# Attention scores as two float16 products over 128 rows instead of one float32 product over 64 rows, from the fourth chunk on

## The chip, the cores and the metric

The kernel runs on one core of a Trainium2 chip. Its metric is the device time in microseconds (us) of one execution; less is better. Before the change three runs gave 695.9, 698.4 and 699.2 us, with a median of 698.4 us. The five engines that matter are TensorE (PE, with its weight loads listed apart as PEld), VectorE (DVE), ScalarE (ACT), GpSimd (POOL) and SyncE (SP), which here only issues DMAs.

## The reference

Attention with a local window and a few global keys, and then a feed-forward layer with a gate:

```python
scores = scale * np.matmul(q, k.transpose(0, 1, 3, 2))      # q, k, v: 4 x 8 x 768 x 64
scores = scores - slopes[:, None, None] * dist               # dist: distance to the key
scores = np.where(is_global | is_local, scores, -1e9)        # 8 global keys, 96 local ones
a = softmax(scores)
x = (a @ v), heads side by side                              # 3072 x 512
h = x @ w_in                                                 # 512 x 2048
out = (h * tanh(softplus(h))) @ w_out                        # 2048 x 512
```

## The kernel before, in words

The 3072 rows are cut into 12 chunks of 256 rows (3 to each of the 4 batches). A chunk's attention consists of 8 tasks t; one task is a pair of heads for one block of 128 rows. The 8 tasks of a chunk fall into two groups G of 4 tasks (4 heads each), and q and k are loaded group by group (`load_qk`). A task runs through these steps, with the lines of the profile:

- scores (`scores`, L340): PE multiplies q and k of the two heads. The heads lie on partitions 0 to 63 and 64 to 127, the operands are float32, and each head's result goes to its own PSUM tile (`sc0`, `sc1`), of which there is one each. A task sees 256 keys (own block, previous 96 keys, global keys); the first block of a batch sees 128.
- `largest` (L354, DVE): adds the mask `mb` or `mb0`, takes the row maximum and writes A. `exps` (L363, ACT): the exponential.
- `high_a` and `low_a` (L147 on DVE or L149 on ACT, and L153, mostly on POOL): A is split into a high and a low float16 part, `hl`, so that later products need only float16. `turn_a` (L383): a DMA on SP transposes `hl` into `AT`. There are three `hl` buffers, so an `hl` can be written only when the transpose of three tasks earlier has read its own.
- `weigh` (L399, PE): AT times v, two tasks later, into `pav` (in the third chunk into `po`).

When the 8 tasks of a chunk are done, `rows` (L410, DVE) divides by the sum, `high_x` and `low_x` (L421, DVE) split the result, and `turn_x` (L427, SP) transposes it into `xT`.

The feed-forward layer has 8 steps m for each chunk: 24 matmuls of 256 columns (`ph`, L444), a chain of ACT and DVE operations (L451, L455, L459, L463, L467, L471, L475), a split of the result into `gt` (L149, then L153 on POOL), and, two steps later, 12 matmuls of 512 columns (`po`, L493). All these operands are float16 in high and low parts, three products for one.

The order of the work is fixed in two ways. Up to step 23 or so a string, PROGRAM, lists every operation by a letter and a number; all engines, SP among them, take it in that order, and each engine works strictly in its own order. In it `q` is a load of q and k, `X` a transposing DMA of `hl`, `t` is `largest`, `g` is `high_a`, `Q` frees `po`, and `W` is `weigh`. Behind it a loop (`attend`) emits the rest in a simple order, and a scheduler places it on the engines.

Of the kernel before, what the change touches and what calls it, by code (L numbers as in the profile page):

```python
# [11 lines left out]
F16 = mybir.dt.float16  # L12
# [4 lines left out]
ALU = mybir.AluOpType  # L17
# [11 lines left out]

SV = 256.0  # L30
# [84 lines left out]
def windowed(st, tc, loc):  # L115
# [14 lines left out]

    cp = st.enter_context(tc.tile_pool(name="cp", bufs=1))
# [24 lines left out]
    raw = {}  # L156
    vraw = {}
# [3 lines left out]
    def load_qk(G):  # L161
        if G >= 2 * NC:
            return
        ci, g = divmod(G, 2)
        b, c = divmod(ci, NCHB)
        qr = raws.tile([P, GH // 2, CH], F32, name="qr", bufs=4)
        kr = raws.tile([P, GH // 2, KW], F32, name="kr", bufs=4)
        o = OWN if c == 0 else 0
        pairs = slice(g * GH // 2, (g + 1) * GH // 2)
        nc.sync.dma_start(qr, L.qT[b].rearrange("(a j) d s -> (j d) a s", j=2)[:, pairs, c * CH:(c + 1) * CH])  # L170
        for j in range(2):
            half = slice(j * D, (j + 1) * D)
            nc.sync.dma_start(kr[half, :, o:], L.kd[ci, half].rearrange("p (a j) w -> p a j w", j=2)[:, pairs, j, o:])
        raw[G] = (qr, kr)
# [68 lines left out]
    def mask_far(h, other=False):  # L243
        copy(mb[:, h, :], rel, -L.slopes[h] * UNIT, other)

# [86 lines left out]
    def scores(t):  # L332
        ci, g, blk, a2, first, nk = shape(t)
        qr, kr = raw[2 * ci + g]
# [3 lines left out]
        for j in range(2):  # L338
            half = slice(j * D, (j + 1) * D)
            nc.tensor.matmul(sc[j][:, 0:w], qr[half, a2, blk * P:(blk + 1) * P], kr[half, a2, col0:col0 + w], start=True, stop=True)  # L340
        pend[t] = sc

    def largest(t):
# [7 lines left out]
        for j in range(2):  # L351
            h = g * GH + 2 * a2 + j
            m = mb0[:, h, :] if first else mb[:, h, :]
            nc.vector.tensor_tensor_reduce(out=A[:, j, 0:w], in0=sc[j][:, 0:w], in1=m, scale=-1.0 / UNIT, scalar=3.0e38, op0=ALU.add, op1=ALU.min, accum_out=nm[:, h:h + 1])  # L354
# [159 lines left out]
    def flags():  # L514
# [12 lines left out]
        "h": high_v, "l": low_v, "x": window_v,  # L527
# [20 lines left out]
        s17 l3 t17 G12 g16' H12 p16' y17 E30 E31 Z6 i7 s18 o6 g17 t18 s19 j7 z12 m7 u7 y18 i13 g18 n7 r7 v4 x3 X16 p17 X17 q7 Z12 p18 X18 t19 s20  # L548
        y19 G7 H7 j13 z7 t20 Z7 m13 u13 g19 y20 p19' o12 s21 o7 i14 n13 g20 t21 s22 r13 y21 g21 X19 G13 p20' H13 t22 Q0 y22 p21 q8 z13' g22' p22'
# [243 lines left out]
```

## Time and profile before

| what | us |
|---|---|
| median of the three runs | 698.4 |
| the profiled execution | 697.84 |
| its span on the core | 695.7 |
| matmul busy (PE) | 630.9 |
| ACT busy | 472.6 |
| DVE busy | 449.2 |
| POOL busy | 266.3 |

The time of an execution is the span from the first to the last instruction and some 2 us around it. In the span matmuls overlap each other, so the mean of one matmul record is longer than the step from one to the next; where a length is needed, the starts of consecutive rows are taken. A row of the timeline gives the start, the length, the engine, the line, what is written from what is read, how many instructions were merged, and in brackets the idle time before it with what ended it. In the groups, "x" is a count, "|" stands ahead of busy us and the mean ns of one.

### The profile page before, as it was taken

To read this page: it belongs to the slowest core of one execution; us is meant where nothing else is said; L and a number is where in the kernel's file an instruction comes from. 1 tells how busy PE (TensorE), PEld (TensorE's weight loads), DVE (VectorE), ACT (ScalarE), POOL (GpSimd) and SP (SyncE) were. 2 spreads that over 40 slices of the span, in tenths; PEclk is the share of its full clock that TensorE was granted. 3 is DMA by queue.
4 is the path that set the end of the run, shared out by engine and by line. 5 is a ranking of instruction groups with operands and counts; after the bars stand their busy time and mean duration, and the time that the engine had idled before them with its cause. 6 is when DMAs were issued, how large, how long until landed. Compare 5 with 4: busy or idle time off the path is not lost.

```text
span 695.7 us, 13412 instructions
## 1 busy us (share of the span) xinstructions
PE 630.9 (91%) x4898; PEld 407.1 (59%) x4898; DVE 449.2 (65%) x1129; ACT 472.6 (68%) x1034; POOL 266.3 (38%) x222
## 2 busy tenths in 40 slices
PE   5556886799799999999999999999999999999993
PEld 3334554456377566666666666666666666666661
DVE  6699989976568647557556566566466565554441
ACT  6576686687577577776776776776776777765652
POOL 1456545642252244344334443443334433331120
PEclk9957899999899999999999999999999999999997
DMA  8999864456444437734435434554444324230000
GB/s 209 201 267 260 255 216 136 149 115 132 108 125 89 116 107 152 144 91 112 116 94 119 96 104 91 118 113 100 109 93 85 69 61 61 77 48 15 31 1 35
DMA packets 152681, 80.38 MB, mean 116 GB/s; under 512 B 121376, under 2 KB 141856, under 8 KB 152608
## 3 DMA queue, kind: packets, MB, share of 16 engines
q1 hardware_dynamic: 152608, 79.46, 48.5%
q8 instruction: 40, 0.66, 0.4%
q14 instruction: 33, 0.27, 0.1%
HBM read 38.54 MB, written 6.29 MB: 64 GB/s over the span
## 4 chain that ended last, share of the span: by engine, by line
ACT 32%; DVE 31%; PE 21%; issue 10%; DMA 4%; POOL 2%; SPq 1%; DVEq 0%; POOLq 0%; ACTq 0%
PE ph L444 9%; DVE e L455 8%; PE po L493 7%; ACT r L463 6%; DVE r L471 6%; ACT u L459 5%; ACT r L467 5%; ACT gt L149 5%; ACT e L451 4%; ACT A L363 3%; DVE gf L475 3%; DVE ws L295 3%; PE sc L340 2%; DVE ws L294 2%; PE pav L493 2%
## 5 line engine op out<-in xcount | busy, mean ns | idle before, releaser
L444 PE MATMUL ph<-xT,wts 128*128 128x256 f16 x2304 | 275.0, 277 | 18.2 <-DVE gmax L475 14.2
L444 PEld LDWEIGHTS <-wts 128*128 128x128 f16 x2304 | 223.9, 99 | 55.2 <-issue 18.5
L493 PE MATMUL po<-wts,gt 128*128 128x512 f16 x1056 | 244.7, 381 | 4.2 <-ACT gt L149 2.7
L153 POOL TENSOR_TENSOR hl<-A,hl 128x512 f16<-128x512 f32 (+1 forms) x90 | 106.6, 1185 | 268.9 <-issue 127.4
L493 PEld LDWEIGHTS <-gt 128*128 128x128 f16 x1152 | 112.3, 99 | 127.6 <-issue 6.4
L153 POOL TENSOR_TENSOR gt<-gf,gt 128x512 f16<-128x512 f32 x93 | 119.6, 1286 | 117.6 <-ACT gt L149 108.6
L471 DVE TENSOR_TENSOR r<-r,e 128x512 f32<-128x512 f32 x96 | 71.8, 748 | 113.3 <-ACT r L467 113.1
L459 ACT ACTIVATE u<-e 128x512 f32<-128x512 f32 x96 | 60.3, 628 | 97.6 <-DVE e L455 97.6
L363 ACT ACTIVATE A<-A,nm 128x256 f32<-128x256 f32 (+1 forms) x192 | 92.0, 480 | 31.2 <-DVE nm L354 30.9
L455 DVE TENSOR_SCALAR e<-e 128x512 f32<-128x512 f32 x96 | 75.7, 789 | 48.6 <-ACT e L451 48.0
L354 DVE CUSTOM_DVE_ANT_0 A<-sc,mb 128x256 f32<-128x256 f32 (+1 forms) x192 | 71.8, 395 | 50.7 <-PE sc L340 48.5
L340 PE MATMUL sc<-kr,qr 64*128 64x256 f32 (+1 forms) x384 | 77.6, 453 | 21.5 <-DVE nm L354 15.7
L149 ACT ACTIVATE gt<-gf 128x512 f16<-128x512 f32 x91 | 57.1, 627 | 40.4 <-DVE gmax L475 40.1
L340 PEld LDWEIGHTS sc<-kr,qr 64*128 64x128 f32 x384 | 37.7, 205 | 58.7 <-DVE nm L354 22.8
L463 ACT ACTIVATE r<-u,quarter 128x512 f32<-128x512 f32 x96 | 69.0, 719 | 2.4
L475 DVE CUSTOM_DVE_ANT_0 gf<-r,ph 128x512 f32<-128x512 f32 x96 | 65.5, 682 | 4.7 <-DVE r L471 2.1
L467 ACT ACTIVATE r<-r 128x512 f32<-128x512 f32 x96 | 60.3, 628 | 2.5
L451 ACT ACTIVATE e<-ph 128x512 f32<-128x512 f32 x96 | 55.8, 581 | 6.8 <-PE ph L444 6.6
L399 PEld LDWEIGHTS <-AT 128*128 128x128 f16 x1056 | 37.8, 100 | 38.2 <-issue 21.0
L153 POOL TENSOR_TENSOR wts<-ws,wts 128x512 f16<-128x512 f32 x32 | 42.0, 1322 | 30.7 <-ACT wts L149 27.1
L399 PE MATMUL pav<-vc,AT 128*128 128x64 f16 x432 | 32.0, 198 | 12.6 <-DMA AT<-hl 11.6
L147 DVE TENSOR_SCALAR hl<-A 128x512 f16<-128x512 f32 (+1 forms) x72 | 36.5, 507 | 4.4 <-ACT A L363 1.9
(82 smaller groups left out, 392.4 us busy)
## 6 DMA issues: line engine op xcount, KB each, us to landing
wts<-w_in SPq DMA_DIRECT2D x16, 512.0 KB, 5.2
wts<-w_out SPq DMA_DIRECT2D x15, 512.0 KB, 5.6
kr<-kd SPq DMA_DIRECT2D x32, 208.0 KB, 3.8
qr<-qT SPq DMA_DIRECT2D x24, 256.0 KB, 3.2
vr<-v SPq DMA_DIRECT2D x12, 512.0 KB, 4.8
out<-ob SPq DMA_DIRECT2D x11, 512.0 KB, 2.9
vc<-vo SPq DMA_DIRECT2D x20, 192.0 KB, 2.8
kr<-kd SPq DMA_DIRECT2D x16, 144.0 KB, 4.0
```

Of the source, the lines that this page charges most:

```text
L149: nc.scalar.activation(out, in_, AF.Copy, scale=scale)
L153: (nc.vector if other else nc.gpsimd).tensor_tensor(out, in_, high, op=ALU.subtract)
L340: nc.tensor.matmul(sc[j][:, 0:w], qr[half, a2, blk * P:(blk + 1) * P], kr[half, a2, col0:col0 + w], start=True, stop=True)
L363: nc.scalar.activation(A[:, j], A[:, j], AF.Exp, bias=nm[:, h:h + 1], scale=-1.0, accum_out=rs[:, h:h + 1])
L444: nc.tensor.matmul(ph[:, j, :].rearrange("p (b t) -> p b t", b=2), wv4[:, 2 * fb, x, c * P:(c + 1) * P], xT[:, :, y * NCC + c, :], start=( ...
L455: nc.vector.tensor_scalar(e, e, NTOP, 0.5, op0=ALU.min, op1=ALU.add)
L459: nc.scalar.activation(u, mish[m]["e"], AF.Square)
L463: nc.scalar.activation(mish[m]["r"], mish[m]["u"], AF.Ln, bias=quarter, scale=1.0 / RS)
L467: nc.scalar.activation(r, r, AF.Exp, scale=-1.0)
L471: nc.vector.tensor_tensor(r, r, mish[m]["e"], op=ALU.mult)
L475: nc.vector.tensor_tensor_reduce(out=gf, in0=mish[m]["r"], in1=mish[m]["h"], scale=SG / (SV * SW * RS), scalar=0.0, op0=ALU.mult, op1=ALU. ...
L493: nc.tensor.matmul(pos[ci][t], gt[:, x, j, t * P:(t + 1) * P], wv4[:, 2 * fb + 1, y, :], start=(fb == 0 and n == 0), stop=(fb == NFB - 1 a ...
```

## The change

From the fourth chunk on (`CF32 = 3`; tasks 24 to 95, groups 6 to 23) the scores are made of float16 products. q and k of a head are loaded twice, onto partitions 0 to 63 and 64 to 127 (`qd`, `kd`, which hold both copies in memory). q, times 256, is split so that the upper copy keeps the high float16 part and the lower copy the rest (`qs`); k is split into a high part `kh` and a rest `kl`, each on all 128 partitions. One matmul over 128 partitions with `kh` then gives (high + low of q) times high of k, and a second one with `kl` is added to it in PSUM. The masks are multiplied by 256 once (`units`, N in PROGRAM), since the scores are. The first three chunks keep the float32 form.

Each group so gets five operations more: `high_q` (a in PROGRAM), `low_q` (b, DVE), `high_k` (c), and `low_k` in two halves (d and e, 832 columns each). Behind PROGRAM `high_q` is on ACT, `high_k` on DVE, and `low_k` on POOL. The PSUM tiles change too: both heads' scores lie in one tile `sc`, and there are two such tiles in place of one pair. The float32 buffers `qr` and `kr` are now two of twice the size in place of four, and a group's load is one DMA for q and one for k, each with twice the bytes.

```diff
+    CF32 = 3
...
+        qr = raws.tile([P, GH, CH], F32, name="qr")
+        kr = raws.tile([P, GH, KW], F32, name="kr")
+        nc.sync.dma_start(qr, L.qd[ci, :, g * GH:(g + 1) * GH, :])
+        nc.sync.dma_start(kr[:, :, o:], L.kd[ci, :, g * GH:(g + 1) * GH, o:])
+        split[G] = (qr, kr) + tuple(stk.tile([P, GH, n], F16, name=m) for m, n in (("qs", CH), ("kh", KW), ("kl", KW)))
...
+    def low_q(G):
+        qr, qs = split[G][0], split[G][2]
+        nc.vector.scalar_tensor_tensor(qs[D:P], qr[D:P], SQ, qs[D:P], op0=ALU.mult, op1=ALU.subtract)
...
+    def split_qk(G):
+        if CF32 <= G // 2 < NC:
+            high_q(G)
+            high_k(G, True)
+            low_q(G)
+            low_k(G, 0, False)
+            low_k(G, 1, False)
...
+        for m in (mb0, mb):
+            nc.vector.tensor_scalar(m, m, SQ, None, op0=ALU.mult)
...
-        sc = [ps.tile([P, W], F32, name=f"sc{j}", bufs=1) for j in range(2)]
-        for j in range(2):
-            half = slice(j * D, (j + 1) * D)
-            nc.tensor.matmul(sc[j][:, 0:w], qr[half, a2, blk * P:(blk + 1) * P], kr[half, a2, col0:col0 + w], start=True, stop=True)
...
+            both = ps.tile([P, 2, W], F32, name="sc")
+            sc = [both[:, j] for j in range(2)]
+            for j in range(2):
+                hh = 2 * a2 + j
+                for n, kk in enumerate((kh, kl)):
+                    nc.tensor.matmul(sc[j][:, 0:w], qs[:, hh, blk * P:(blk + 1) * P], kk[:, hh, col0:col0 + w], start=(n == 0), stop=(n == 1))
...
-            if ta % 4 == 0:
+            if ta % 4 == 1:
                 load_qk(ta // 4 + 1)
...
+            if ta % 4 == 3:
+                split_qk(ta // 4 + 1)
```

What this does to the order is shown at three places. The first is PE, at the scores of one late task; `pav` and `po` are the neighbours. Before, the two float32 products of a task stand as two rows, without loads of their own:

```order
L493 MATMUL po1_2918<-wts_102,gt_2750 128x512
L340 MATMUL sc0_2939<-kr_2151,qr_2150 128x256
L340 MATMUL sc1_2940<-kr_2151,qr_2150 128x256
L399 LDWEIGHTS AT_2782
L399 MATMUL pav0_2688<-vc_2648,AT_2782 128x64
```

and now as four loads and four products, into one tile:

```order
L392 LDWEIGHTS qs_2179
L392 MATMUL sc_2979<-kh_2180,qs_2179 128x256
L392 LDWEIGHTS qs_2179
L392 MATMUL sc_2979<-kl_2181,qs_2179 128x256
L392 LDWEIGHTS qs_2179
L392 MATMUL sc_2979<-kh_2180,qs_2179 128x256
L392 LDWEIGHTS qs_2179
L392 MATMUL sc_2979<-kl_2181,qs_2179 128x256
```

Only what is written and read has changed; the place between `po` and `pav` is the same here.

The second place is SP in PROGRAM, at the load of group 7 (`q7`), which stands between the transposes of tasks 16, 17 and those of tasks 18, 19. Before:

```order
L383 DMA_TRANSPOSE AT_1650<-hl_1544 128x8x128
L383 DMA_TRANSPOSE AT_1653<-hl_1595 128x8x128
L170 DMA qr_1655<-qT 128x2x256
L173 DMA kr_1656<-kd 64x2x288 x2
L383 DMA_TRANSPOSE AT_1662<-hl_1640 128x8x128
L383 DMA_TRANSPOSE AT_1761<-hl_1687 128x8x128
L170 DMA qr_1776<-qT 128x2x256
```

and now:

```order
L435 DMA_TRANSPOSE AT_1647<-hl_1540 128x8x128
L435 DMA_TRANSPOSE AT_1650<-hl_1591 128x8x128
L183 DMA qr_1652<-qd 128x1024
L184 DMA kr_1653<-kd 128x4x288
L435 DMA_TRANSPOSE AT_1661<-hl_1636 128x8x128
L435 DMA_TRANSPOSE AT_1764<-hl_1689 128x8x128
L183 DMA qr_1779<-qd 128x1024
```

The order is the same, but the load into `qr_1652` now reuses the buffer of group 6 and waits for DVE's `low_q` of that group (b7, which stands in PROGRAM behind t21); the next one, into `qr_1779`, waits for the scores of task 23 on PE. The two transposes of tasks 18 and 19 stand behind the first of these waits.

The third place is DVE at the end of chunk 6's attention, from the division `x` to the low part of `xhl`, which the transpose into `xT` waits for. Before:

```order
L410 ISA x_4525,xmax_105<-pav1_4105,ri_4523 128x512
L410 ISA xmax_105 128x1
L475 ISA gf_4479,gmax_106<-r_4475,ph_4445 128x512
L475 ISA gmax_106 128x1
L191 SCALAR_TENSOR_TENSOR vo_4907<-vr_4662,vo_4907 128x2x512
L147 TENSOR_SCALAR hl_4505<-A_4500 128x512
L421 TENSOR_TENSOR xhl_4527<-x_4525,xhl_4527 128x512
```

and now:

```order
L462 ISA x_4620,xmax_105<-pav1_4181,ri_4618 128x512
L462 ISA xmax_105 128x1
L150 TENSOR_SCALAR hl_4600<-A_4595 128x512
L527 ISA gf_4566,gmax_106<-r_4562,ph_4532 128x512
L527 ISA gmax_106 128x1
L150 TENSOR_SCALAR hl_4689<-A_4684 128x512
L229 SCALAR_TENSOR_TENSOR vo_5013<-vr_4758,vo_5013 128x2x512
L473 TENSOR_TENSOR xhl_4622<-x_4620,xhl_4622 128x512
```

The `hl` of a second task has come in between, since with two PSUM tiles the scheduler lets the scores of two tasks follow each other here. On SP the transposes of both tasks now stand ahead of the one into `xT`:

```order
L239 DMA vc_5016<-vo_4336 96x1024
L240 DMA vc_5016<-vc_4339 32x1024 x2
L435 DMA_TRANSPOSE AT_4603<-hl_4600 128x8x128
L435 DMA_TRANSPOSE AT_4692<-hl_4689 128x8x128
L479 DMA_TRANSPOSE xT_4450<-xhl_4622 128x8x128
```

where before `xT` came ahead of the transpose of its neighbour task.

More of the change, by code (lines that the diff above doesn't have):

```diff
@@ L28 @@
 RS = 2.0 ** 8
+SQ = 256.0
 SV = 256.0
@@ L526, in windowed @@
         "q": load_qk, "v": load_v, "w": load_w,
-        "h": high_v, "l": low_v, "x": window_v,
+        "a": lambda p, other=False: high_q(p - 1, other), "b": lambda p: low_q(p - 1), "c": lambda p, other=False: high_k(p - 1, other),
+        "d": lambda p, other=False: low_k(p - 1, 0, not other), "e": lambda p, other=False: low_k(p - 1, 1, other), "N": units, "h": high_v, "l": low_v, "x": window_v,
         "K": lambda i: masks_far() if i else masks_own(), "L": mask_own, "M": mask_far,
```

63 lines of the change are left out of this document (43 added, 20 removed).

## The prediction

> **What bounds the kernel now.** I read the shares of the engines first, then the busy time by stretch, since an average over 696 us hides the stages, then the waits of PE, then the timeline of one period. The shares, from the page:
>
> ```profile
> PE 630.9 (91%) x4898; PEld 407.1 (59%) x4898; DVE 449.2 (65%) x1129; ACT 472.6 (68%) x1034; POOL 266.3 (38%) x222
> ```
>
> and four stretches (length, then busy us of each engine, granted PE clock, DMA share, GB/s):
>
> ```profile
> core 0: us, PE busy (x) PEld busy (x) DVE busy (x) ACT busy (x) POOL busy (x), PEclk, DMA share, GB/s
> 0.00:70.00 70.00, 40.01 (x276) 26.90 (x277) 57.30 (x160) 46.04 (x121) 33.37 (x34) 0.80 1.02 235
> ...
> 140.00:200.00 60.00, 55.23 (x447) 34.02 (x446) 36.48 (x117) 42.26 (x112) 18.90 (x18) 0.93 0.55 123
> ...
> 380.00:440.00 60.00, 60.00 (x493) 39.03 (x491) 36.88 (x99) 42.75 (x94) 23.23 (x19) 1.00 0.48 104
> ...
> 620.00:680.00 60.00, 58.69 (x399) 37.70 (x396) 25.63 (x47) 34.83 (x60) 12.71 (x11) 1.00 0.05 14
> ```
>
> Until about 140 us other things than PE set the pace, and the change does nothing there. From 200 us on PE is busy all the time, at the full granted clock, and its recorded waits are tiny (longest rows of 200 to 420 us and of 420 to 640 us: total, times, longest):
>
> ```profile
> PE ph L444 <- DMA xT<-xhl: 0.3, 1, 0.3
> ...
> PE pav L399 <- DMA AT<-hl: 1.3, 2, 1.1
> ```
>
> A busy PE need not be a PE at its limit, so I check one period by the starts of its rows:
>
> ```profile
> 403.18 0.70 PE L340 MATMUL sc<-kr,qr 64*128 64x256 f32 x4
> 403.82 0.26 PE L399 MATMUL pav<-vc,AT 128*128 128x64 f16 x3
> ...
> 404.18 2.78 PE L444 MATMUL ph<-xT,wts 128*128 128x256 f16 x24
> 406.80 2.75 PE L493 MATMUL po<-wts,gt 128*128 128x512 f16 x12
> 409.48 0.70 PE L340 MATMUL sc<-kr,qr 64*128 64x256 f32 x4
> ```
>
> 24 `ph` matmuls take 2.62 us (109 ns for 256 columns), 12 `po` 2.68, `pav` 0.36, the scores of one task 0.64 us, and the next period starts at once. So in the stage where 64 of the 72 changed tasks run, what PE saves is saved, as long as nothing else becomes late.
>
> **The scores.** A changed task has four float16 products of 256 columns. The nearest row is `ph`: float16, 128 rows, 256 columns, each with its own load of 128 columns, 109 ns in all. That makes 0.44 us in place of 0.64, a gain of 0.20 us. If loads weren't hidden (the page gives them a mean of 99 ns), it would be 4 x 0.208 = 0.83 us, a loss of 0.19; `ph` has just these loads, hidden, so I take 0.44. Twelve tasks (first blocks of three batches) have 128 columns:
>
> ```profile
> 165.03 0.26 PE L399 MATMUL po<-vc,AT 128*128 128x64 f16 x3
> ...
> 176.98 0.25 PE L399 MATMUL po<-vo,AT 128*128 128x64 f16 x3
> 181.06 1.56 PE L340 MATMUL sc<-kr,qr 64*128 64x256 f32 x4 [3.83 <-DVE nm L354]
> 182.55 6.95 PE L493 MATMUL pav<-wts,gt 128*128 128x512 f16 x24
> 189.43 0.49 PE L340 MATMUL sc<-kr,qr 64*128 64x128 f32 x4
> 189.86 2.79 PE L444 MATMUL ph<-xT,wts 128*128 128x256 f16 x24
> ```
>
> They take 0.43 us (189.43 to 189.86) and will take half of 0.44. Sum: 60 x 0.20 + 12 x 0.21 = **-14.7 us**.
>
> **The splits.** The page's rows for such conversions and subtractions:
>
> ```profile
> L147 DVE TENSOR_SCALAR vo<-vr 128x1024 f16<-128x1024 f32 x1 | 0.7, 689 | 0.0
> ...
> L191 DVE SCALAR_TENSOR_TENSOR vo<-vr,vo 128x1024 f16<-128x1024 f32 x12 | 15.6, 1297 | 0.0
> ...
> L149 ACT ACTIVATE vo<-vr 128x1024 f16<-128x1024 f32 x11 | 11.5, 1044 | 0.1
> ...
> L153 POOL TENSOR_TENSOR hl<-A,hl 128x512 f16<-128x512 f32 x75 | 95.5, 1273 | 234.1 <-issue 115.7 <-PE po L493 42.5 <-ACT hl L149 31.6
> ...
> L153 POOL TENSOR_TENSOR hl<-A,hl 128x256 f16<-128x256 f32 x15 | 11.2, 746 | 34.7 <-issue 11.6 <-ACT hl L149 11.4 <-PE ph L444 6.7
> ```
>
> For each of the 18 groups: `high_q` 1.04 us on ACT; `high_k`, 1664 columns, 0.689 x 1.625 = 1.1 us on DVE; `low_q` 1.3 on DVE; `low_k` twice 832 columns on POOL, by the slope of the last two rows (0.53 us for 256 columns) 1.27 + 320 x 0.0021 = 1.93 each, 3.9 in all. The masks cost once 3072 columns, 2.1 us of DVE. In 60 us there are 2.4 groups: DVE goes from 36.9 to 42.7 us, ACT from 42.8 to 45.3, POOL from 23.2 to 32.5, while PE falls from 60 to 58. No engine passes PE, so the work itself costs nothing; what it can cost is lateness at a place where PE waits for a chain.
>
> **The loads.** A row each for k (two DMAs of a late group) and for q:
>
> ```profile
> kr<-kd SPq DMA_DIRECT2D x32, 208.0 KB, 3.8
> qr<-qT SPq DMA_DIRECT2D x24, 256.0 KB, 3.2
> ...
> AT<-hl SPq DMA_TRANSPOSE x96, 2.8
> ...
> xT<-xhl SPq DMA_TRANSPOSE x24, 3.5
> ```
>
> A group's 672 KB become 1344 KB. At 104 GB/s a period of 60 us moves 6.2 MB; 2.4 groups add 1.6 MB, a quarter, so the DMA share goes from 0.48 to some 0.60. That is free as bandwidth. A transpose issued just behind a load may land 2 to 3 us later (672 KB at the 235 GB/s of the first stretch). Ahead of the transposes stand now two waits for splits (below).
>
> The Trainium skill, in "DMA: Bandwidth & Descriptors", Queues, rings and completion order, says that each DMA engine consumes the descriptors of a ring in order. By that rule the 2 to 3 us are the whole delay of the transposes behind a doubled load; the rows here show no transpose behind so large a load.
>
> **PROGRAM's stretch, 140 to 200 us.** One wait goes: PE stood still from 177.1 to 181.06 for the only pair of score tiles (task 27 waits until DVE has read task 26). With two tiles it passes, and the `po` rows that began at 182.55 may begin up to 4.9 us earlier. What is late next is behind SP's new wait (SP, DVE, ACT):
>
> ```profile
> 151.66 0.58 SPq L170 DMA_DIRECT2D qr<-qT  x1
> ...
> 153.86 7.21 SPq L383 DMA_TRANSPOSE AT<-hl  x2
> ...
> 160.02 0.42 DVE L354 CUSTOM_DVE_ANT_0 A<-sc,mb 128x256 f32<-128x256 f32 x1
> ...
> 162.69 0.63 ACT L149 ACTIVATE hl<-A 128x512 f16<-128x512 f32 x1
> 163.22 0.58 ACT L500 ACTIVATE ob<-po 128x512 f32<-128x512 f32 x1
> ```
>
> Group 7's load went out at 151.66, task 18's transpose at 153.86. Now the load waits for b7, which follows t21 (until 160.4) and takes 1.3 us: 161.7 at the earliest. Issuing takes 1.2 us, so the transpose starts at 162.9 and lands at 165.7 to 168. ACT's `hl` of task 21 (162.69) needs that buffer, and behind it ACT frees `po` (163.22), for which task 16's `weigh` waits on PE (165.03). It starts at 167 to 169.5, 2 to 4.5 us late. Later transposes, queued behind group 8's load (which waits for task 23's scores), add up to 2. Of the 4.9 us most is so lost: between -4.5 and +2 us, and I take **-2.0**.
>
> **The end of each chunk.** The feed-forward steps of a chunk need `xT`, whose chain starts at the chunk's last `weigh`. One such end before:
>
> ```profile
> 423.07 2.78 PE L444 MATMUL ph<-xT,wts 128*128 128x256 f16 x24
> ...
> 425.51 0.68 DVE L410 CUSTOM_DVE_ANT_1 x<-pav,ri 128x512 f32<-128x512 f32 x1
> ...
> 427.86 1.38 DVE L147 TENSOR_SCALAR hl<-A 128x512 f16<-128x512 f32 x1
> ...
> 429.16 0.68 DVE L421 TENSOR_TENSOR xhl<-x,xhl 128x512 f16<-128x512 f32 x1
> 429.87 1.24 SPq L427 DMA_TRANSPOSE xT<-xhl  x1
> ...
> 435.67 1.58 PE L444 MATMUL ph<-xT,wts 128*128 128x256 f16 x13
> ```
>
> and, from the groups, the mean of such an `hl`:
>
> ```profile
> L147 DVE TENSOR_SCALAR hl<-A 128x512 f16<-128x512 f32 x63 | 31.9, 507 | 4.0 <-ACT A L363 1.9 <-DMA AT<-hl 0.5
> ```
>
> The last `weigh` ends at 423.07; the transpose goes out 6.8 us later and lands 3.5 after that, at 433.4; PE wants it at 435.67. There are 2.3 us to spare, of 12.6. In the new order I add up PE's work between these two points with the steps above: 13.1 us for the fifth chunk, 10.8 to 12.3 for the later ones, as the scores are shorter and some were moved forward. The chain meanwhile gets longer where a second task has come between: its maxima (0.84 us) and its `hl` (0.51, or 1.38 as above) on DVE, and its transpose (1.24) ahead of `xT` on SP. That is 12 to 13.5 us against 10.8 to 11 at three ends, about +1.5 each, and little at the other six: **+5.5 us**, between 0 and 13.5 (1.5 at all nine).
>
> DVE also slows down beside POOL: the `hl` at 427.86 took 1.38 us while POOL was at work, against a mean of 0.51. POOL gets 9.3 us more in 60, so such rows become more frequent; that lies within the bounds just given.
>
> The Trainium skill, in "GPSIMD Engine Reference", section 1 (Specifications), says that POOL shares its SBUF interfaces with VectorE and contends with VectorE's two-port modes and two-input operations. The 1.38 us agree. It speaks against this change, which gives both engines more of such work, and would be a reason for the second rival.
>
> **The sum.** Against the profiled execution (697.84, its span of 695.7 and 2.1 around it): 697.8 - 14.7 - 2.0 + 5.5 = **686.6 us**. That execution lies 0.6 below the median of the three runs, 698.4. The forecast's own range is 682 to 692.
>
> **The rivals.**
>
> - *Nothing is lost.* The chains stay ahead, as their 2.3 us of spare time and DVE's 20 us of slack in 60 allow, and the gap at 177 us closes almost whole: 697.8 - 14.7 - 4.5 = 678.6. Against it speaks the new order on SP.
> - *The gain is eaten at the chunk ends*: 1.4 us at each of nine ends and nothing gained in PROGRAM's stretch: 697.8 - 14.7 + 12.6 = 695.7. For it speaks that PE has less to do in the meantime, everywhere but in one place.
> - *`xT` becomes the bound.* If the second task's DVE work (0.84 + 1.38), two transposes ahead (2.5) and 2.5 for a doubled load in front all add to the 10.3 us, the chain takes 17.5 against 12.3 or less; with half of it hidden, 3 us are lost at nine ends: 697.8 - 14.7 + 27 = 710. It decides once a chunk's end loses over 2.1 us (18.8 in all, for 0.5% above the median). Against it: most ends show only part of this.
> - *The change doesn't speed the scores up.* If the loads of `qs` aren't hidden, a task takes 0.83 us: 697.8 + 72 x 0.19 = 711.5. Against it speaks `ph`.
>
> **How the numbers follow.** Forecast 0.64, nothing lost 0.13, eaten 0.14, `xT` as the bound 0.05, slow products 0.04. The likeliest is 686.6. The range of 679 to 696.5 takes in the first three almost whole, with the bounds of PROGRAM's stretch (-4.5 to +2) and of the chunk ends (0 to 13.5) about the sum, and leaves out the last two. A measurement of this kernel tells about 0.5% from no change (694.9 to 701.9). Faster than that are the forecast and the first rival, 0.77; within it the second, 0.14; slower the last two, 0.09.
>
> **What would show it.** In the profile after: four `sc` records of a late task within 0.44 us, with the next row at once; PE's waits for `xT` or for `AT` after 200 us at 3 to 8 us in all (near 0: first rival; over 12: second); no wait of `sc` for `nm` at 177 us, but one of the task 16 `weigh` for ACT before 170. DVE should be near 43 us in a stretch of 60 and POOL near 33. The prediction is wrong if a row of `sc` costs more than 0.11 us, if PE waits for the splits themselves (`sc` on POOL's `kl`), or if the granted clock after 200 us is below 1.00.

## The result and the profile after

Slower: 742.0 us (median of four runs, 741.2 to 742.5) against 698.6 us (four runs, 695.9 to 699.2), a ratio of 1.063, with a 95% interval of 1.060 to 1.066. The profiled execution took 742.36 us, its span 740.6. The forecast was 686.6, its range 679 to 696.5, and none of the rivals reached 742 either.

The shares of the engines, from the page of the kernel after:

```profile
PE 625.1 (84%) x4898; PEld 421.2 (57%) x4898; DVE 522.5 (71%) x1168; ACT 482.8 (65%) x1052; POOL 335.4 (45%) x257
```

PE does less in more time; DVE has 73 us more than before, POOL 69. The same stretches as before, and two more, show where PE now stands still (length, then busy us of each engine, granted PE clock, DMA share, GB/s):

```profile
140.00:200.00 60.00, 49.87 (x362) 30.15 (x361) 39.75 (x104) 38.87 (x96) 26.02 (x19) 0.86 0.51 118
...
260.00:320.00 60.00, 48.60 (x392) 33.80 (x391) 47.01 (x101) 37.37 (x86) 33.88 (x24) 0.94 0.74 186
...
380.00:440.00 60.00, 54.39 (x456) 37.63 (x455) 42.19 (x93) 40.42 (x88) 30.35 (x21) 1.00 0.46 115
...
560.00:620.00 60.00, 54.48 (x464) 37.73 (x463) 44.75 (x105) 41.66 (x92) 31.93 (x22) 1.00 0.42 82
620.00:680.00 60.00, 59.35 (x493) 41.34 (x491) 34.04 (x83) 40.57 (x86) 21.64 (x18) 1.00 0.31 58
```

From 200 to 620 us PE is idle 4.5 to 6 us in every 60, once 11, while there are splits to do, and nearly full again behind that. The granted clock, 1.00 in each of these stretches from 200 us on before, is 0.94 from 260 to 320 us. To place the loss I use the moment at which ACT begins to empty a chunk's `po` (`evacuate`), here for chunks 1, 2 and 9, first in the kernel before, then after:

```profile
188.25 0.60 ACT L500 ACTIVATE ob<-pav 128x512 f32<-128x512 f32 x1 [4.26 <-PE pav L493]
...
245.89 0.58 ACT L500 ACTIVATE ob<-po 128x512 f32<-128x512 f32 x1
...
598.70 0.58 ACT L500 ACTIVATE ob<-po 128x512 f32<-128x512 f32 x1
```

```profile
198.78 0.58 ACT L552 ACTIVATE ob<-pav 128x512 f32<-128x512 f32 x1
...
257.83 0.58 ACT L552 ACTIVATE ob<-po 128x512 f32<-128x512 f32 x1
...
643.56 0.58 ACT L552 ACTIVATE ob<-po 128x512 f32<-128x512 f32 x1
```

Up to chunk 1 (PROGRAM's stretch) 10.5 us are lost, to chunk 2 another 1.4, and in chunks 3 to 9, that is from the second row to the third, 385.7 us stand against 352.8: **32.9 us lost** where 14.7 us of scores less were to be gained. This length, "chunks 3 to 9", is used below for every run, since PROGRAM's stretch varies by some 5 us from one execution to the next. What PE waits for between 260 and 640 us (total, times, longest):

```profile
PE ph L496 <- DVE gmax L527: 29.9, 19, 5.7
PE pav L451 <- DMA AT<-hl: 6.0, 7, 1.6
PE ph L496 <- DMA xT<-xhl: 1.1, 1, 1.1
PE po L545 <- POOL gt L156: 1.0, 2, 0.6
```

Four fifths are `ph` waiting for `gmax`, the end of `times_h`: a step's matmuls need the PSUM tile that `times_h` of two steps earlier reads. In the same window the kernel before waited 1.6 us in all, and never for `gmax`. One place where it arises, with the engines in order of time (rows between these left out):

```profile
388.96 1.03 DVE L150 TENSOR_SCALAR kh<-kr 128x1664 f16<-128x1664 f32 x1 [1.58 <-PE sc L392]
...
390.14 3.94 POOL L156 TENSOR_TENSOR kl<-kr,kh 128x832 f16<-128x832 f32 x2 [1.74 <-DVE kh L150]
...
391.20 1.25 DVE L523 TENSOR_TENSOR r<-r,e 128x512 f32<-128x512 f32 x1
...
392.48 2.67 DVE L195 SCALAR_TENSOR_TENSOR qs<-qr,qs 64x1024 f16<-64x1024 f32 x1
...
394.26 0.27 PE L392 MATMUL sc<-kh,qs 128*128 128x256 f16 x1
394.37 0.27 PE L392 MATMUL sc<-kl,qs 128*128 128x256 f16 x1
394.48 0.27 PE L392 MATMUL sc<-kh,qs 128*128 128x256 f16 x1
394.59 0.27 PE L392 MATMUL sc<-kl,qs 128*128 128x256 f16 x1
394.69 0.25 PE L451 MATMUL pav<-vc,AT 128*128 128x64 f16 x3
...
395.60 0.68 DVE L527 CUSTOM_DVE_ANT_0 gf<-r,ph 128x512 f32<-128x512 f32 x1
...
396.32 0.63 ACT L152 ACTIVATE gt<-gf 128x512 f16<-128x512 f32 x1 [3.81 <-DVE gmax L527]
```

The scores are what was predicted, 0.11 us a product, 0.43 a task. But between the end of `r` (392.45) and `gf` (395.60), which lie at most 0.9 us apart in the kernel before (200 to 640 us), stands `low_q`, which takes 2.67 us. And it takes so long because of `low_k` on POOL: the first half of `low_k` is held by nothing and ends at about 391.9; `r`, begun meanwhile, ends 0.55 us later; then the second half, which waited for `r`, ends at 394.08, and `low_q` ends 1.07 us behind it. ACT waits 3.81 us for this. The groups of the whole span (busy us, mean ns, idle before):

```profile
L523 DVE TENSOR_TENSOR r<-r,e 128x512 f32<-128x512 f32 x96 | 86.4, 900 | 90.4 <-ACT r L519 89.9
...
L195 DVE SCALAR_TENSOR_TENSOR qs<-qr,qs 64x1024 f16<-64x1024 f32 x18 | 36.4, 2025 | 6.9 <-ACT qs L152 6.4
```

`low_q` was put at 1.3 us and takes 2.03; `r` had 748 ns before.

### The profile page after: what moved, and what is told of

Read it like the earlier page. It is cut to its first block, busy times and chain, and to the rows that moved or that the text cites. A ratio compares the mean times of both kernels' runs of the same rounds, so it can differ in the third digit from the quotient of the medians.

```text
span 740.6 us, 13462 instructions
## 1 busy us (share of the span) xinstructions
PE 625.1 (84%) x4898; PEld 421.2 (57%) x4898; DVE 522.5 (71%) x1168; ACT 482.8 (65%) x1052; POOL 335.4 (45%) x257
## 4 chain that ended last, share of the span: by engine, by line
DVE 35%; ACT 21%; PE 19%; DMA 11%; issue 11%; POOL 1%; SPq 1%; DVEq 0%; ACTq 0%; POOLq 0%
PE ph L496 8%; DMA AT<-hl 7%; DVE r L523 7%; PE po L545 7%; DVE e L507 6%; ACT r L515 4%; DVE gf L527 4%; ACT u L511 4%; DVE qs L195 3%; ACT r L519 3%; ACT gt L152 3%; DVE A L406 3%; ACT A L415 2%; DVE ws L338 2%; DVE ws L337 2%
## 5 line engine op out<-in xcount | busy, mean ns | idle before, releaser
L496 PE MATMUL ph<-xT,wts 128*128 128x256 f16 x2304 | 284.6, 282 | 56.0 <-DVE gmax L527 52.4
L496 PEld LDWEIGHTS <-wts 128*128 128x128 f16 x2304 | 227.5, 101 | 101.0 <-DVE gmax L527 36.1
L156 POOL TENSOR_TENSOR hl<-A,hl 128x512 f16<-128x512 f32 (+1 forms) x90 | 111.5, 1241 | 201.4 <-issue 68.7
L156 POOL TENSOR_TENSOR gt<-gf,gt 128x512 f16<-128x512 f32 x93 | 117.9, 1268 | 135.9 <-ACT gt L152 115.8
L523 DVE TENSOR_TENSOR r<-r,e 128x512 f32<-128x512 f32 x96 | 86.4, 900 | 90.4 <-ACT r L519 89.9
L507 DVE TENSOR_SCALAR e<-e 128x512 f32<-128x512 f32 x96 | 71.2, 742 | 33.8 <-ACT e L503 33.6
L406 DVE CUSTOM_DVE_ANT_0 A<-sc,mb 128x256 f32<-128x256 f32 (+1 forms) x192 | 68.1, 393 | 24.1 <-PE sc L392 11.8
L156 POOL TENSOR_TENSOR kl<-kr,kh 128x832 f16<-128x832 f32 (+1 forms) x35 | 65.7, 1894 | 24.8 <-DVE kh L150 20.0
L451 PEld LDWEIGHTS <-AT 128*128 128x128 f16 x1056 | 43.9, 102 | 43.3 <-DMA AT<-hl 26.7
L384 PE MATMUL sc<-kr,qr 64*128 64x256 f32 (+1 forms) x96 | 29.1, 599 | 16.7 <-DVE nm L406 10.5
```

What stands on the lines that cost most here:

```text
L156: (nc.vector if other else nc.gpsimd).tensor_tensor(out, in_, high, op=ALU.subtract)
L496: nc.tensor.matmul(ph[:, j, :].rearrange("p (b t) -> p b t", b=2), wv4[:, 2 * fb, x, c * P:(c + 1) * P], xT[:, :, y * NCC + c, :], start=( ...
L507: nc.vector.tensor_scalar(e, e, NTOP, 0.5, op0=ALU.min, op1=ALU.add)
L523: nc.vector.tensor_tensor(r, r, mish[m]["e"], op=ALU.mult)
```

## The experiments

Each time is that of one execution; the kernel before ran beside them, group by group, with 698.6, 698.1, 697.8, 699.7 and 694.7 us. Small differences between single executions tell nothing: the kernel before alone spreads over 5 us. In chunks 3 to 9 it is less; the kernel after, e8_lowq_first and e11, whose DVE, ACT and PE turned out to have the very same order of operations, lie within 2.2 us there. "Chunks 3 to 9" is worked out from the rows of `ob` as above, and "DVE busy" is DVE's busy time in just this stretch. e1 to e6 and e17 leave some of the work out.

| run | edit to the kernel after | us | chunks 3 to 9 | DVE busy |
|---|---|---|---|---|
| (before) | | 697.8 | 352.8 | 215.4 |
| (after) | | 742.4 | 385.7 | 276.4 |
| e1_none | no loads, no splits from group 10 on | 686.1 | 335.3 | 212.0 |
| e2_loads | loads, no splits | 692.3 | 342.1 | 214.5 |
| e3_splits | splits, no loads | 725.6 | 372.9 | 268.5 |
| e4_nolowk | all but `low_k` | 699.9 | 347.8 | 243.3 |
| e5_lowk_only | `low_k` alone | 704.0 | 342.0 | 220.1 |
| e6_iota_only | iotas on POOL instead | 689.5 | 335.2 | 212.1 |
| e7_lowk_dve | `low_k` on DVE | 743.9 | 390.2 | 278.0 |
| e8_pieces | `low_k` in four pieces | 732.1 | 379.0 | 265.9 |
| e17_half | half of `low_k` | 723.5 | 368.4 | 264.4 |
| e8_lowq_first | `low_q` ahead of `high_k` | 738.8 | 386.8 | 275.4 |
| e13_spread | splits over three tasks | 738.6 | 382.1 | 270.2 |
| e16_custom_r | other form of `r` | 738.0 | 386.5 | 275.9 |
| e9_ph3 | three `ph` tiles | 735.6 | 380.4 | 273.9 |
| e18_lag3 | and one step more of lag | 735.2 | 383.2 | 276.5 |
| e11_q7 | q7 later in PROGRAM | 735.2 | 387.9 | 275.1 |
| e14_combo | spread, pieces and q7 | 721.7 | 376.9 | 264.7 |
| e15_packed | half the split work, old loads | 706.3 | 356.9 | 243.5 |
| e19_packed_dve | and `low_k` on DVE | 695.3 | 349.0 | 237.7 |

### Which part costs it: e1 to e4

In all four, groups from 10 on take operands of groups 8 and 9 where their own are not made.

```diff
 e1_none: in load_qk, and split_qk does nothing
+        if G >= 10:
+            split[G] = split[8 + G % 2]
+            return
 e2_loads: the same lines behind the two DMAs
 e3_splits
+        if G >= 10:
+            split[G] = split[8 + G % 2][:2] + tuple(stk.tile(...) for ...)
+            return
 e4_nolowk
-            low_k(G, 0, False)
-            low_k(G, 1, False)
```

> Left out: from group 10 on (chunk 5 on) q and k are neither loaded nor split; the scores are the same float16 products on the operands of groups 8 and 9. Theory (the splits stand in ACT's and DVE's order ahead of the feed-forward chain, ph's two PSUM tiles come free late, PE waits): the stage after 200 us runs as predicted, i.e. 198.4 (first ph of chunk 2 in the changed kernel) + 505.8 (before, from there to the end) - 12 to 13 of scores + 2 = 693 to 695 us, and PE's wait of ph for gmax falls from 52 to about 20 us. Rival 'order' (two score tiles and the new order of the tasks themselves cost the time, not splits or loads): 735 to 742. Rival 'loads': also 693.

> Left out: from group 10 on the doubled loads are kept and nothing is split; the scores use the operands of groups 8 and 9. Theory (splits): as without loads, 693 to 697 us. Rival 'loads' (the doubled bytes delay the transposes): 725 to 742, with PE's waits for AT as in the changed kernel (about 17 us). Rival 'order': 735 to 742.

> Left out: from group 10 on the loads; the splits are all done, on the float32 operands of groups 8 and 9, which are there already. Theory (splits in front of the chain, whether their load is late or not): 725 to 738 us. Sub-rival (only splits that wait for late loads hurt, in-order waiting): 695 to 705. Rival 'loads': 693 to 697.

> Left out: from group 10 on low_k (POOL); loads, high_q, high_k and low_q are kept, and the products take kl of groups 8 and 9. Theory with the order on ACT and DVE as main part: 720 to 735 us. Rival 'POOL' (DVE's rows stretch beside low_k, and that is what makes the chain late): 693 to 705, with low_q back at about 1.2 us a row.

Without loads and splits the time is 686.1, without splits alone 692.3: the products and the order of the tasks are not what costs, the rivals "loads" and "order" fall. Against the kernel before, the scores and the doubled loads together gain 352.8 - 342.1 = 10.7 us in chunks 3 to 9. `high_q`, `high_k` and `low_q` add 5.6 (347.77 against 342.13), and **`low_k` adds 38.0** (385.73 against 347.77). Of these 38.0 PE is idle for 29.4 and busy for 8.6, with the same number of products (347.4 us of PE for 338.8): behind some of its waits it runs at half the clock (last section). DVE's order differs in part between these runs, so each difference holds some of that too. With it gone, `low_q` and `r` are short again (260 to 640 us):

```profile
L524 DVE TENSOR_TENSOR r<-r,e 128x512 f32<-128x512 f32 x62 | 44.1, 711 | 55.2 <-ACT r L520 54.8
...
L198 DVE SCALAR_TENSOR_TENSOR qs<-qr,qs 64x1024 f16<-64x1024 f32 x14 | 17.8, 1271 | 3.3 <-ACT qs L152 2.9
```

My theory, which put the main part on ACT's and DVE's own splits, had expected 720 to 735 there; the rival "POOL" had it. The late loads cost little: with resident operands (e3) 12.8 of 43.6 us go, 6.8 of them by e1 and e2 the loads' own.

### POOL's queue, or DVE and POOL excluding each other: e5, e6, e7

```diff
 e5_lowk_only (split_qk; on top of e1_none)
+                nc.gpsimd.tensor_tensor(junk..., kr[:, hs, o:], kh[:, hs, o:], op=ALU.subtract)
 e6_iota_only (split_qk; on top of e1_none)
+            for i in range(6):
+                nc.gpsimd.iota(junk, pattern=[[1, KW]], ...)
 e7_lowk_dve
-            low_k(G, 0, False)
-            low_k(G, 1, False)
+            low_k(G, 0, True)
+            low_k(G, 1, True)
```

> Left out from group 10 on: loads, high_q, high_k and low_q (the scores use the operands of groups 8 and 9). Kept: low_k alone, twice 832 columns on POOL for each group, into a scratch buffer that nothing reads, so no product waits for it. Theory 'exclusion' (an operation of DVE on SBUF operands and one of POOL never run at the same time: the later one waits for the other's end): 695 to 715 us, against 686.1 without it; DVE rows r and e that begin beside a low_k end 0.55 and 0.28 us behind its end; rows that read PSUM (gf, A) keep 0.68 and 0.41. Rival 'POOL queue' (low_k stands ahead of hl's and gt's low parts on POOL, and these become late): also above 690, but r stays at 0.69 and PE's added waits are for AT or for gt. Rival 'only together' (low_k costs only because low_q and high_k stand in front of it on DVE): below 689.

> As the run with low_k alone, but POOL instead writes six iotas of 416 float32 columns for each group (about 4 us of POOL, nothing read). Rival 'POOL queue': the same time as with low_k alone, within 4 us. Theory 'exclusion': by the first iotas of the kernel nothing can be said of whether an iota excludes DVE too; if it doesn't, r and e stay as in the run with nothing (686 to 688 us); if it does, each piece holds DVE for at most 0.7 us instead of 1.77, and the time lies between 686 and the run with low_k alone.

> Nothing left out; behind PROGRAM low_k is on DVE instead of POOL (14 groups, two rows of 832 columns, by r's 0.69 for 512 about 1.1 us each). Theory 'exclusion': the run without low_k (699.9) plus at most 14 x 2.2 = 31 us, of which DVE's idle time hides about half or more: 700 to 716 us, faster than the changed kernel although DVE gets more work; low_q near 1.25 us a row. Rival 'DVE is too full' (what matters is DVE's work ahead of the chain): 740 or more.

`low_k` alone, which no product waits for, costs 17.9 us (704.0 against 686.1). DVE and ACT have the very same operations in the very same order in both runs. As nothing held `low_k` back, it ran in a bunch between 194 and 297 us, so chunks 3 to 9 show only a part; PE had 48.1 busy us from 200 to 260, against 54.1 in e6. From the `ob` of chunk 1 to that of chunk 3 the same 188 operations of DVE take 103.2 busy us instead of 78.7, and the stretch 126.0 instead of 107.9. PE's added waits there are for `gmax` (3.4 us), for the transposes of `hl` (5.6) and for POOL's `gt` (2.9), so POOL's queue has some part of its own, which these runs don't separate. The iotas, some 47 us of POOL, come out 3.4 above e1, no more than single executions differ by; but they had run before 200 us, most of them where PE doesn't set the pace, so the total doesn't answer the rival "POOL queue". What this run does answer stands in the rows. DVE beside eleven iotas (162.23 to 168.18 us):

```profile
163.54 1.22 DVE L198 SCALAR_TENSOR_TENSOR qs<-qr,qs 64x1024 f16<-64x1024 f32 x1
164.79 0.69 DVE L524 TENSOR_TENSOR r<-r,e 128x512 f32<-128x512 f32 x1
```

```profile
162.23 5.95 POOL L212 IOTA junk<- 128x416 f32 x11
```

`low_q` and `r` aren't touched by a POOL that only writes; beside `low_k`, which reads, they wait for its end. The Trainium skill, in "SBUF — State Buffer", Who interferes with whom, says just this: a VectorE instruction with two SBUF inputs contends with a GpSimd instruction that reads SBUF, not with one that only writes, and the later of the two is blocked for the whole instruction. The trace agrees (0.69 and 1.22 us beside iotas, 1.25 and 2.67 beside `low_k`).

But POOL as such isn't the cause: on DVE, where it can't hold other rows of DVE from POOL, `low_k` costs as much (743.9; 390.2 in chunks 3 to 9). My expectation was wrong by 28 us. The last column of the table says why. Without `low_k` DVE is busy for 243.3 us of chunks 3 to 9; with `low_k` on POOL for 276.4, though DVE has the same 611 operations, and with `low_k` on DVE for 278.0. What counts is the time that `low_k` takes from DVE, be it in DVE's own order or by POOL's. That the two times agree so closely is partly luck, since the order differs: in e7 the scheduler put the splits of eight of the 14 groups into chunks 3 and 4 (five in the kernel after), where 143.8 us stand against 117.3, and chunks 5 to 9 are faster than in the kernel after, 246.4 against 268.5.

### Length, spare time, place: e8_pieces, e17, e8_lowq_first, e13, e16

```diff
 e8_pieces (low_k)
-        rest(split[G][4][:, hs, o:], ...)
+        for h in range(half * GH // 2, (half + 1) * GH // 2):
+            rest(split[G][4][:, h, o:], ...)
 e17_half: low_k(G, 1, False) only for G < 10; heads 2 and 3 use kh in place of kl
 e8_lowq_first (split_qk): low_q(G) ahead of high_k(G, True)
 e13_spread (attend): load at ta % 4 == 0; high_q, high_k at 1; low_q, half of low_k at 2; the rest at 3
 e16_custom_r (times_r)
-        nc.vector.tensor_tensor(r, r, mish[m]["e"], op=ALU.mult)
+        nc.vector.tensor_tensor_reduce(out=r, in0=r, in1=mish[m]["e"], ..., op0=ALU.mult, op1=ALU.max, accum_out=rmax)
```

> Nothing left out; low_k is done in four pieces of 416 columns for each group instead of two of 832 (same engine, same bytes, also in the written order). Theory 'exclusion': DVE waits for one piece (about 0.97 us) instead of one half (1.77) each time, r beside low_k falls from 1.6 to about 1.2 us, and the time from 742 to 718 to 735. Rival 'POOL queue': POOL's total grows by some 0.4 us for each group, so 742 or a little more.

> Left out from group 10 on: low_k of two of a group's four heads (their second product uses kh in place of kl). Cost in proportion: 742 - 21 = 721 us. Theory 'spare time' (only what exceeds some 2 to 3 us of a step's spare time costs): clearly less than half of the 42 us is left, 702 to 714.

> Nothing left out; behind PROGRAM low_q is written ahead of high_k, so that low_k, which needs high_k, can't run beside it. Theory 'exclusion': low_q falls from 2.08 to about 1.25 us a row, 14 x 0.8 = 11 us less in the clumps, 728 to 735 us. Rival (DVE's whole time in the clump counts, low_q's wait only covers what another row would wait): r, hl or e wait in its place, 738 to 744.

> Nothing left out; behind PROGRAM a group's load is emitted one task earlier and its splits are emitted over three tasks (high_q and high_k, then low_q and half of low_k, then the other half) instead of together. Theory (the clump of some 5 to 6 us ahead of the feed-forward chain exceeds its spare time of about 2.5 us, single pieces mostly don't): 700 to 720 us, PE's waits of ph for gmax below 30 us. Rival (the work itself, wherever it stands): 735 to 742.

> Nothing left out; r times e (two SBUF operands, TENSOR_TENSOR) is done by tensor_tensor_reduce, the form that gf and A have (these never stretched beside POOL, but also read PSUM). If the form is what is exempt: r at 0.69 to 0.75 us a row also beside POOL, 0.08 more for its accumulator, and the time falls to 720 to 735. If the SBUF operands are what counts: r still ends about 0.55 us behind POOL's end, and the time is 742 to 748.

Shorter pieces gain 6.7 us in chunks 3 to 9 (10 in the whole), as exclusion would have it, although POOL is busy for longer there (210.8 us for 193.7); for the rival "POOL queue" the time should have grown. Half of `low_k` leaves 20.6 of its 38.0 us (368.4 - 347.8), 54%, with 21.0 us more of DVE (264.38 against 243.35): the cost of `low_k` goes by its length, and my "spare time" of a step is not there for it. It was there for the splits ahead of it: `high_k` and `low_q` add 28.8 us to DVE (243.3 - 214.5) and cost 5.6. In all 15 runs with splits, whatever DVE has to do (237.7 to 278.0 us), it is idle for 104 to 113 us of chunks 3 to 9, against 127.6 without splits (e2, time less DVE busy): 14 to 24 us of its idle time could be filled, and no run filled more. In the same way `low_k` costs 17.9 us alone (e5) and 38.0 beside the other splits. The order differs between most of these runs, so this is a regularity over them and not a test of its own. By POOL's own pace (1.77 us for a half that is held by nothing, 390.14 to 391.91 above; at most 49.6 us for 14 groups), some three quarters of `low_k` turn into time (38.0 of 49.6).

e8_lowq_first tells nothing: the scheduler, which places what the loop emits, put every operation of DVE, ACT, POOL and PE in the very same order as in the kernel after (at 388.8 us `low_q` again takes 2.67), so its 738.8 is one more time of that kernel. e13_spread has another order only until some 360 us; chunks 3 and 4 gain 7 us by it (110.3 for 117.3), and chunks 5 to 9, in the old order, take 271.7 for 268.5. So spreading was tested only in part. The time of e16, 738.0, lies between its two ranges and answers nothing, but its rows show that the form isn't what exempts `gf` and A: `r` in their form still ends 0.55 us behind POOL's first half (here at 416.74) and takes 1.94.

```profile
415.35 1.94 DVE L524 CUSTOM_DVE_ANT_0 r<-r,e 128x512 f32<-128x512 f32 x1 [0.68 <-ACT r L520]
```

```profile
414.96 3.94 POOL L156 TENSOR_TENSOR kl<-kr,kh 128x832 f16<-128x832 f32 x2
```

The 0.68 of `gf`, which reads one operand from PSUM, is the same beside POOL as alone.

### Is it the tile that comes free late: e9, e18

```diff
-        ph = ps.tile([P, 2, CH], F32, name="ph")
+        ph = ps.tile([P, 2, CH], F32, name="ph", bufs=3)
-            both = ps.tile([P, 2, W], F32, name="sc")
+            both = ps.tile([P, 2, W], F32, name="sc", bufs=1)
 e18_lag3 also: four gt buffers behind PROGRAM, and
-    MOELAG = 2
+    MOELAG = 3
```

> Nothing left out; ph gets three PSUM tiles and the float16 scores one tile instead of two (there are eight banks), and PROGRAM's scores 26 to 33 stand behind the maxima of the task before again; in the first three chunks the second head's scores take turns in ph's tiles. Theory 'ph comes free late' (a step's matmuls wait for times_h of two steps earlier, and the splits push times_h back by more than its spare time): with a third tile there are some 6 us more to spare in each step, the waits of ph for gmax fall from 52 us to 20 or less, and behind 260 us most of the loss is gone; the stage from the evacuation of chunk 3 to that of chunk 11 (404.6 us in the changed kernel, 388.6 before) takes 375 to 388 us. Rival 'ACT, DVE or POOL are simply full': it stays near 400 us, the waits move to AT, gt or sc.

> Nothing left out; as the run with three ph tiles, and behind PROGRAM the second matmuls of a feed-forward step come three steps later instead of two, with four gt buffers. If the cost is latency of one step's chain: the 30 us of waits for gt go, and chunks 3 to 9 (380.3 us in the run with three ph tiles, 352.8 before) take 345 to 360 us, 700 to 716 in all. If DVE and POOL together are full: 375 us or more, 730 to 736, with waits elsewhere.

The waits of `ph` for `gmax` are gone, and the time nearly stays (380.4 and 383.2 us in chunks 3 to 9, for 385.7). PE's waits from 260 to 640 us, first with three tiles, then with a lag of three steps:

```profile
PE po L545 <- ACT gt L152: 10.7, 5, 5.0
PE po L545 <- POOL gt L156: 9.6, 12, 1.6
PE pav L451 <- DMA AT<-hl: 9.5, 8, 2.9
```

```profile
PE pav L451 <- DMA AT<-hl: 27.8, 15, 4.6
PE sc L392 <- DVE nm L406: 4.8, 3, 3.2
```

Some 30 to 35 us of waits in all each time, and each time the next thing that comes out of the same row of DVE, ACT and POOL: `gt` first, then `hl` and its transpose. The tile was where the wait showed, not its cause. More room between PE and these engines doesn't help; DVE is idle for 107 us in chunks 3 to 9 both times, as in the kernel after (109).

### PROGRAM's stretch: e11, and the edits together: e14

```diff
-... X17 q7 Z12 p18 X18 ... b7 X19 G13 ...
+... X17 Z12 p18 X18 ... b7 X19 q7 G13 ...
```

> Nothing left out; in PROGRAM the load of group 7 (q7) stands behind the transpose of task 19 instead of ahead of that of task 18. Theory (SP's wait for low_q in front of task 18's transpose costs 8.5 us in PROGRAM's stretch): the first ph of chunk 2 is at 189 to 193 us instead of 198.4, task 16's weigh no longer waits 5.8 us for ob, and the total falls by 5 to 9 us, to 733 to 737. Rival (something else in that stretch, such as the added splits on ACT and DVE): 740 to 743.

> Nothing left out; the three edits together: splits spread over three tasks, low_k in pieces of 416 columns, q7 behind task 19's transpose. If all three theories hold, their gains mostly add: 690 to 710 us. If the clump isn't the cause: about 725 (10 from the pieces, 6 to 8 from q7).

In the kernel after, the chain that was feared stands in the rows of SP, ACT and PE:

```profile
150.37 2.63 SPq L435 DMA_TRANSPOSE AT<-hl  x2
163.53 0.34 SPq L183 DMA_DIRECT2D qr<-qd  x1
163.98 0.38 SPq L184 DMA_DIRECT2D kr<-kd  x1
164.40 5.61 SPq L435 DMA_TRANSPOSE AT<-hl  x2
```

```profile
171.25 0.63 ACT L152 ACTIVATE hl<-A 128x512 f16<-128x512 f32 x1 [7.11 <-DMA AT<-hl]
171.78 0.58 ACT L552 ACTIVATE ob<-po 128x512 f32<-128x512 f32 x1
```

```profile
172.50 0.32 PE L451 MATMUL po<-vc,AT 128*128 128x64 f16 x3 [5.80 <-ACT ob L552]
```

The load leaves at 163.53 and not at 161.7, task 18's transpose lands at 171.2, 6.8 us after its issue where 2.8 was the median. With q7 behind task 19's transpose `po` of chunk 1 is emptied at 189.7 instead of 198.8 (twelve other runs with the same PROGRAM: 193.5 to 198.7; before 188.3), and the whole takes 6.8 us less than the median after, 3.6 less than e8_lowq_first. Nothing is gained against before, though the wait of scores for maxima near 177 us is gone: in its place stands

```profile
176.06 0.34 PE L451 MATMUL po<-vc,AT 128*128 128x64 f16 x3 [5.58 <-DMA AT<-hl]
```

behind the next load. e14 adds the pieces' and q7's gains, 721.7 for the 725 expected of them; what spreading adds beside the pieces can't be told (110.7 us in chunks 3 and 4, 111.7 with the pieces alone).

### Half the work: e15, e19

q and k of two heads are loaded once, side by side on 64 partitions each, as before the change. They are split in that layout, with half the columns, and a head takes three products over 64 partitions.

```diff
+            for n, (x, kk) in enumerate(((0, kh), (1, kh), (0, kl))):
+                for j in range(2):
+                    half = slice(j * D, (j + 1) * D)
+                    nc.tensor.matmul(sc[j][:, 0:w], qs[half, x, a2, ...], kk[half, 0, a2, ...], start=(n == 0), stop=(n == 2))
 e19_packed_dve (split_qk)
-            low_k(G, 0, False)
-            low_k(G, 1, False)
+            low_k(G, slice(0, GH // 2), True)
```

> Nothing left out; another layout: q and k of two heads lie on 64 partitions each, as before the change, loaded once; high and low parts are made in that layout (each split operation has half the columns) and a head's scores are three float16 products over 64 partitions, in two banks as before. PROGRAM's scores stand behind the maxima of the task before. Clump theory: with half the split work (ACT 0.6, DVE 0.6 + 0.7, POOL 2 x 0.97 for a group) the chain keeps its spare time, so 14 groups cost 0 to 8 us; the scores take 6 x 0.109 = 0.65 us a task if products on different rows of the array don't overlap (0.64 before), or about 0.33 if they do. So 697 to 706 us, or 680 to 692. Rival (any split work ahead of the chain costs in proportion): half of 50 us more, 720 or above.

> Nothing left out; the packed layout, with low_k behind PROGRAM as one operation of 832 columns on DVE (1.1 us by r's 0.69 for 512) instead of two of 416 on POOL (1.9 us). If what counts is the length in front of the chain, whichever engine: 14 x 0.8 = 11 us less than the packed run's 706.3, about 695. If moving it to DVE gains nothing, as in the run with low_k on DVE: 704 to 710.

One task of e15_packed, and the row behind it:

```profile
405.58 0.39 PE L385 MATMUL sc<-kh,qs 64*128 64x256 f16 x4
405.81 0.27 PE L385 MATMUL sc<-kl,qs 64*128 64x256 f16 x2
406.01 0.26 PE L444 MATMUL pav<-vc,AT 128*128 128x64 f16 x3
```

Six products take 0.43 us, as long as four over 128 rows. So they overlap, and for that case 680 to 692 us were expected; that 706.3 lies at the upper end of the other range, for products that don't, is luck. The splits still cost some 15 us in chunks 3 to 9 (356.9 against 342.1 in e2, which has twice the loads). With `low_k` on DVE, where it is one operation of 1.1 us instead of two on POOL of 1.13 on average, it is 695.3 and 349.0, as expected from the length. So here DVE was the better place, and in the layout of the change (e7) it was not; DVE's busy time went with it, 243.5 to 237.7 us here, 276.4 to 278.0 there. The kernel before took 694.7 us beside it, no difference that can be told: no version that does all of the work was faster than the kernel before.

## Why the prediction was wrong

- **The scores** (-14.7; the factors as printed give 14.5): right. Four products take 0.44 us, and chunks 3 to 9 became 10.7 us shorter where nothing is split (e2).
- **The splits**: here it failed. "No engine passes PE, so the work itself costs nothing; what it can cost is lateness at a place where PE waits for a chain." DVE at 42 to 47 of 60 us and POOL at 30 to 34 in the stretches above are near the forecast of 42.7 and 32.5, but being below PE didn't make the work free: it cost 43.6 us in chunks 3 to 9 (385.7 - 342.1), 38.0 of them `low_k`. Two assumptions were wrong. DVE and POOL were added up as two engines, while operations of both on SBUF operands exclude each other: `low_k` on POOL took 33.1 us of DVE's time in chunks 3 to 9. And DVE's idle time was taken for spare time, while most of it is the waiting between links of a chain (ACT, DVE, ACT three times, DVE twice, ACT, POOL) in a fixed order: of 127.6 idle us no run with splits used more than 24. That what is put between two links delays all that follow is seen at the one place above and argued for the rest. The page of the kernel before had a hint of it: the chain of work that ended last, followed back from the last instruction, runs through ACT and DVE for 63% of the span and through PE for 21%, although PE is busy for 91%.

```profile
ACT 32%; DVE 31%; PE 21%; issue 10%; DMA 4%; POOL 2%; SPq 1%; DVEq 0%; POOLq 0%; ACTq 0%
```

- The row that showed the exclusion was in the prediction: an `hl` of 1.38 us beside POOL, with the Trainium skill's "GPSIMD Engine Reference", section 1, that speaks against the change. It was priced inside the bounds of the chunk ends, 0 to 13.5 us. `low_q` was mis-sized, 2.03 us for 1.3, for the same reason.
- **The end of each chunk** (+5.5): the wrong chain. I looked for what PE waits for at nine chunk ends (`xT`); those waits are 1.1 us from 260 to 640. The 29.9 us came up within the chunks, at `ph` behind `times_h`, which I never checked for its spare time.
- **PROGRAM's stretch** (-2.0, between -4.5 and +2): the chain was right, the size wrong, +10.5 in this execution and +5.2 to +10.5 in the thirteen with this PROGRAM. The load left 1.8 us later than I had put it, the transposes behind it landed after 6.8 instead of 3 to 5, and the 4.9 us of the closed gap were not gained, since the 5.80 us of `weigh` at 172.50, behind a transpose, took its place. PE also ran at a lower clock here, 0.86 for 0.93.
- **The rivals**: "gain eaten at the chunk ends" and "`xT` becomes the bound" named a mechanism that hardly occurred; "scores not faster" didn't occur. None was for lateness of the feed-forward chain itself.
- **The signs**: PE's waits for `xT` and `AT` after 200 us are 8.7 us, hardly over the 3 to 8 forecast, `sc` takes 0.11 us a product at the full clock, and PE doesn't wait for POOL's `kl`. These signs were tied to the wrong chain and would almost have passed the prediction. One sign of being wrong did come up, the granted clock below 1.00 after 200 us.

The sum, of the spans: 10.5 (to chunk 1) + 1.4 + 32.9 (chunks 3 to 9) + 0.1 behind = 44.9 us.

What stays open: why the scheduler bunched the splits in e7, and so what `low_k` on DVE costs in the order of the kernel after; how much of `low_k`'s 38.0 us goes by POOL's own queue; and whether another order would hide the splits. Of the two edits that were to change the order, one left it as it was and one changed only its beginning.

## What to carry to other kernels

An engine's idle time is free only if it isn't the waiting inside a chain that the bound engine depends on: before adding work to a helper engine, take the tightest chain through it, put the new operations between its links, and see by how much the last one moves. Here some 14 to 24 of DVE's 127.6 idle us could be filled. Add DVE and POOL up as one engine wherever both work on SBUF operands, as 33.1 us of DVE here were POOL's. If a wait moves on when a buffer is added, the cause lies in the engines that write or empty it.

## What the hardware showed

- DVE and POOL take turns by whole operations. `r` and `low_q` that begin beside a POOL subtraction end 0.55 and 1.07 us behind its end, whatever they take alone (0.69, 1.22), and a POOL operation that begins beside `r` waits for `r` (2.21 us for 1.77 at 391.9 us). Rows of one SBUF operand are held too: `e` and `hl`, 0.42 alone, end 0.28 us behind POOL's end and take up to 1.98. Beside POOL's iotas `r` and `low_q` keep their 0.69 and 1.22, and a row with an operand in PSUM (`gf`, 0.67 to 0.69 in all its rows behind 140 us) is never held.
- After 5.7 us without work PE ran at a granted clock of 0.50 (308.5 to 313 us): `ph` took 5.30 us in place of 2.79, with `sc` at 0.21 us a product behind it. The clock was 0.50 for some 3 us also behind a wait of 2.2 us at 369.0, but 1.00 behind waits of 2.3 and 2.5 us at 325.9 and 478.9, so the length of one wait doesn't tell it.

```profile
308.56 5.30 PE L496 MATMUL ph<-xT,wts 128*128 128x256 f16 x24 [5.69 <-DVE gmax L527]
313.65 0.42 PE L392 MATMUL sc<-kh,qs 128*128 128x256 f16 x1
313.87 0.42 PE L392 MATMUL sc<-kl,qs 128*128 128x256 f16 x1
```

  Such a wait costs more than its length.
- Products over 64 rows on both halves of the array overlap: six take 0.43 us in e15, as long as four over 128 rows.
